# Row halves at the head of an attention and GeGLU kernel: half-width gate/up, and gate and up weights on two queues

## The chip, the cores and the metric

The kernel runs on one core of a Trainium2 chip. A core has a matmul engine (PE, whose weight loads are listed as PEld), a vector engine (DVE), an activation engine (ACT), GpSimd (POOL) and a sync engine (SP), which here only issues DMAs. The engines run side by side, each takes its own instructions in order, and they wait for each other by semaphores. ACT, POOL and SP can issue DMAs, and each of them has a queue of its own; 16 DMA engines work off the queues. The metric is the device time of one execution in microseconds (us): 560.81 as the median of 3 runs (560.77 to 560.82).

## What is computed

The input x has 2048 rows of 448 numbers. With xn = layernorm(x), the result is x + s * silu(g), where s is sliding attention over a key/value cache and g a gated feed-forward block:

```python
xn = _layernorm(x, axis=-1)
s = _A_ref(xn, A_k_cache, A_v_cache, A_wq, A_wo)   # 16 heads of 256, 8 KV heads, last 512 keys
g = _silu(_B_ref(xn, B_w_gate, B_w_up, B_w_down))  # (gelu(xn@w_gate) * (xn@w_up)) @ w_down, F = 1792
return x + s * g
```

Everything is bfloat16 with sums in float32.

## The kernel before, in words

The rows are taken in four chunks of 512 (`QC`), each of four tiles of 128 rows (`TPC`). Every operation goes through a recorder (`Rec`), which is told what an operation reads and writes, keeps the order in which each engine's operations were written, and adds the semaphore waits. So the order of the lines in the kernel is the order on each engine.

There are two stages. In the first, for each chunk, 14 blocks (`NF`) of 128 feed-forward columns run through `gate_up`, and then `down` multiplies by w_down for each of the four row tiles (the last chunk's `down` is put into the gaps of the second stage). The second stage goes over the 64 pairs of chunk and head: scores, softmax, values and output projection. It starts at about 127 us and the change does not touch it.

**`gate_up(c, f)`** (matmuls on line 370). 448 = 7 x 64, so the contraction runs in 7 steps (`NK`) of 64 rows (`HP`). The gate weights stand in partitions 0 to 63 of the tile `wgu`, the up weights in partitions 64 to 127, and the transposed rows `xnT` stand twice, once in either half. One step is two matmuls of 64 rows by 512 columns, one in each half of PE, into two neighbouring PSUM banks. There are three such pairs of banks (`NGB`), used in turn: block f+3 needs the banks of block f. ACT applies gelu to the gate bank (line 374), DVE multiplies the up bank by it (line 376) into `actT`.

**The head**, before the first `gate_up`. SP issues, in this order: the four row tiles of chunk 0; gate and up slices 0 and 1; the rows of chunk 1; gate and up slices 2 and 3; w_down; the rows of chunks 2 and 3. The slices are cut at blocks 0, 2, 6, 10 and 14, so slice 0 serves blocks 0 and 1. A gate slice is one DMA and an up slice another. DVE makes mean and variance of a row tile (lines 288 and 289), ACT the square root of two tiles together (line 330), DVE the reciprocal (line 333) and the normalised rows `xn2` (line 294), PE the 14 transposes of a tile (line 316), and ACT and DVE, tile by tile in turn, copy them from PSUM to `xnT` (lines 322 and 324). Ahead of its transposes PE runs 12 matmuls on zeroed data (`warm`, line 303), whose result nobody reads. A dummy square root on ACT (line 263) has its function table loaded early. Gelu needs another table, whose load stands ahead of the first gelu.

**Chunk 1's rows** are normalised while chunk 0 is in `gate_up`: `ln_later(t)` makes the statistics on DVE and the reciprocal root on POOL (lines 345 and 347), `ln_later2(t)` normalises on DVE and has the rows transposed by a DMA that SP issues (line 236). Eight such calls are hung behind blocks 4 to 11 (`lead = 4`), one behind each block's product, and behind blocks 1 to 8 for the chunks after. POOL also issues the loads of wq, V and wo (`load_piece`), from block 9 on, each after the matmul written last before it.

**`down(c, t)`** (line 382) is 14 matmuls, one for each block f, which reads block f of `actT`. PE takes them in order, so a late product stops it there.

```python
            lead = 4 if c == 0 else 1
            for f in range(NF):
                gate_up(c, f)
                if c + 1 < NQC and lead <= f < lead + 2 * TPC:
                    t, half = divmod(f - lead, 2)
                    (ln_later2 if half else ln_later)((c + 1) * TPC + t)
```

## Time and profile before

| | us |
|---|---|
| median of 3 runs | 560.81 (560.77 to 560.82) |
| the profiled execution | 561.18 |
| its span, first to last instruction | 559.4 |
| PE busy | 549.0 (98%) |
| DVE, ACT, POOL busy | 322.9, 296.1, 90.1 |
| first gate/up matmul starts | 9.26 |
| first down matmul starts | 30.91 |
| first row tile lands; up slices 0, 1, 2, 3 land | 2.77; 7.62, 12.54, 18.49, 22.54 |

Lines of a timeline read: start, duration, engine, line, operation, written tile<-read tiles, shapes, number of instructions merged, and in brackets the idle time of the engine before them with what ended it. A line with many instructions merged lasts from the start of the first to the end of the last. In a table of stretches each engine has its busy time and, in brackets, its number of instructions; the last three numbers are the granted PE clock (1.00 is full), the busy share of the DMA engines and GB/s. In the chain that ended last each piece has its start, its length and what it was.

### The profile page before, as it was taken

How to read it: one execution, taken by the hardware profiler on the slowest of the kernel's cores; microseconds unless marked ns; L12 is line 12 of the kernel's file. 1: busy time of each engine (PE TensorE's matmuls, PEld its weight loads, DVE VectorE, ACT ScalarE, POOL GpSimd, SP SyncE). 2: the span in 40 equal slices, each digit the busy share in tenths (PEclk: the TensorE clock that was granted, in tenths of full speed). 3: DMA queues.
4: the chain of work that ended last, by engine and by line, in shares of the span. 5: the costliest groups of instructions: out<-in, count | busy, mean ns of one | idle time of the engine just before them, and what ended most of it. 6: DMA issues, size and time to landing. Idle time of an engine off the chain costs nothing.

```text
span 559.4 us, 9865 instructions
## 1 busy us (share of the span) xinstructions
PE 549.0 (98%) x3499; PEld 257.2 (46%) x3532; DVE 322.9 (58%) x835; ACT 296.1 (53%) x673; POOL 90.1 (16%) x125
## 2 busy tenths in 40 slices
PE   7999999999999999999999999999999999999997
PEld 3544444444444444444444444444444444444445
DVE  5636446143464847474846657484747484755674
ACT  4324233247655565556565656656565656565641
POOL 0232323200000111013501101232100021400023
PEclk9999999999999999999999999999999999999999
DMA  8994746972453435353664344445535353645352
GB/s 193 276 191 86 138 102 136 247 137 65 94 85 68 97 64 99 69 91 64 143 98 94 73 86 71 81 84 137 101 67 99 63 95 71 147 79 101 70 92 52
DMA packets 169552, 58.83 MB, mean 105 GB/s; under 512 B 160160, under 2 KB 166432, under 8 KB 169504
## 3 DMA queue, kind: packets, MB, share of 16 engines
q1 hardware_dynamic: 166208, 45.50, 44.2%
q0 software_dynamic: 3152, 12.65, 8.9%
q8 instruction: 28, 0.46, 0.4%
q14 instruction: 20, 0.16, 0.1%
q10 hardware_dynamic: 144, 0.06, 0.0%
HBM read 17.92 MB, written 1.84 MB: 35 GB/s over the span
## 4 chain that ended last, share of the span: by engine, by line
PE 95%; DMA 1%; DVE 1%; issue 1%; SPq 1%; ACT 0%
PE ps L440 20%; PE ps L420 19%; PE ps L406 18%; PE ps L460 16%; PE ps L370 15%; PE ps L382 8%; DMA wgu<-in_B_w_up_dram 1%; SPq L233 1%; DVE tmp L469 0%; DVE ofin L471 0%; DVE pr L427 0%; DVE oT L446 0%; DVE rden L426 0%; ACT pr L424 0%
## 5 line engine op out<-in xcount | busy, mean ns | idle before, releaser
L424 ACT ACTIVATE pr<-ps 128x512 bf16<-128x512 f32 x256 | 152.8, 597 | 116.6 <-PE ps L420 112.5
L420 PE MATMUL ps<-kT,qT 128*128 128x512 bf16 x481 | 145.4, 379 | 3.3 <-issue 2.5
L440 PE MATMUL ps<-pT,V 128*128 128x512 bf16 x510 | 130.8, 379 | 0.6 <-DVE rden L426 0.4
L426 DVE RECIPROCAL rden<-den 128x1 f32<-128x1 f32 x256 | 41.5, 162 | 152.4 <-ACT pr L424 134.3
L460 PE MATMUL ps<-wo,oT 128*128 128x448 bf16 (+1 forms) x536 | 116.3, 344 | 0.0
L427 DVE TENSOR_SCALAR pr<-pr,rden 128x512 bf16<-128x512 bf16 x256 | 106.4, 416 | 9.0
L406 PE MATMUL ps<-xnT,wq 64*128 64x512 bf16 x896 | 99.5, 376 | 0.0
L410 ACT ACTIVATE qT<-ps 128x1024 bf16<-128x1024 f32 x64 | 65.5, 1024 | 49.8 <-PE ps L406 49.8
L370 PE MATMUL ps<-xnT,wgu 64*128 64x512 bf16 x784 | 85.5, 376 | 1.0 <-ACT xnT L322 0.8
L446 DVE CAST oT<-ps 128x512 bf16<-128x512 f32 x124 | 84.6, 682 | 0.6 <-PE ps L440 0.5
L440 PEld LDWEIGHTS ps<-pT,V 128*128 128x128 bf16 x512 | 49.9, 98 | 60.8 <-issue 1.2
L460 PEld LDWEIGHTS ps<-wo,oT 128*128 128x128 bf16 x536 | 52.3, 98 | 51.1
L420 PEld LDWEIGHTS ps<-kT,qT 128*128 128x128 bf16 x512 | 48.5, 98 | 57.1 <-issue 7.3
L376 DVE TENSOR_TENSOR actT<-ps,hb 128x512 bf16<-128x512 f32 x56 | 38.1, 685 | 57.5 <-ACT hb L374 55.7
L406 PEld LDWEIGHTS ps<-xnT,wq 64*128 64x128 bf16 x896 | 42.4, 94 | 55.9 <-DVE acc L481 4.2
L374 ACT ACTIVATE hb<-ps 128x512 bf16<-128x512 f32 x56 | 33.4, 597 | 51.8 <-PE ps L370 51.8
L370 PEld LDWEIGHTS ps<-xnT,wgu 64*128 64x128 bf16 x784 | 39.2, 94 | 46.5 <-issue 2.5
L424 ACT ACTIVATION_READ_ACCUMULATOR pr<-ps 128x1 f32 x256 | 49.9, 195 | 0.0
L500 POOL TENSOR_SCALAR tmp<-tmp 128x448 f32<-128x448 f32 x16 | 9.1, 572 | 233.9 <-ACT tmp L499 233.9
L382 PE MATMUL ps<-wd,actT 128*128 128x448 bf16 x224 | 46.2, 353 | 0.1
L485 POOL TENSOR_TENSOR tmp<-acc,gy 128x448 f32<-128x448 f32 x16 | 16.6, 1035 | 123.2 <-DVE acc L481 123.2
L382 PEld LDWEIGHTS ps<-wd,actT 128*128 128x128 bf16 x224 | 21.7, 98 | 22.2 <-issue 1.3
(43 smaller groups left out, 171.7 us busy)
## 6 DMA issues: line engine op xcount, KB each, us to landing
pT<-pr SPq DMA_TRANSPOSE x256, 2.4
wq<-in_A_wq_dram POOLq DMA_DIRECT2D x14, 256.0 KB, 4.3
wo<-in_A_wo_dram POOLq DMA_DIRECT2D x4, 896.0 KB, 10.1
V<-in_A_v_cache_dram POOLq DMA_DIRECT2D x4, 512.0 KB, 5.8
xr<-in_A_x_dram POOLq DMA_DIRECT2D x4, 448.0 KB, 4.8
wd<-in_B_w_down_dram SPq DMA_DIRECT2D x1, 1568.0 KB, 17.6
wgu<-in_B_w_gate_dram SPq DMA_DIRECT2D x3, 448.0 KB, 10.3
wgu<-in_B_w_up_dram SPq DMA_DIRECT2D x3, 448.0 KB, 11.8
```

Of the source, the lines that this page charges most:

```text
L370: ins = e.matmul(bank(b), lhsT=wgu[lo:lo + HP, k, f * P:(f + 1) * P], rhs=xnT[lo:lo + HP, c, k, :], start=k == 0, stop=k == NK - 1)
L376: dve(lambda e: e.tensor_tensor(actT[:, f, :], bank(s + 1), hb[:, n % NHB, :], ALU.mult), r=[("ps", s + 1), ("hb", n % NHB)], w=[("actT", f)])
L382: pe(lambda e, f=f: e.matmul(bank(b, D), lhsT=actT[:, f, t * P:(t + 1) * P], rhs=wd[:, f, :], start=f == 0, stop=f == NF - 1), r=[("actT", ...
L406: ins = e.matmul(bank(b), lhsT=wq[lo:lo + HP, k, h0 // 2 + hp, e_ * P:(e_ + 1) * P], rhs=xnT[lo:lo + HP, c, k, :], start=k == 0, stop=k == ...
L410: act(lambda e, e_=e_, s=s, i=i: e.activation(qT[:, i:i + 2, e_, :], psum[:, s * 512:(s + 2) * 512].rearrange("p (a q) -> p a q", a=2), AC ...
L420: ins = e.matmul(bank(b), lhsT=qT[:, i % 6, k, t * P:(t + 1) * P], rhs=kT[:, g, k, :], start=k == 0, stop=k == NE - 1)
L424: act(lambda e: e.activation(pr[s][:, :], bank(b), ACT.Exp, scale=scale, accum_out=den[:, s:s + 1]), r=[("ps", b)], w=[("pr%d" % s,), ("de ...
L426: dve(lambda e: e.reciprocal(rden[:, s:s + 1], den[:, s:s + 1]), r=[("den", s)], w=[("rden", s)])
L427: dve(lambda e: e.tensor_scalar(pr[s][:, :], pr[s][:, :], rden[:, s:s + 1], None, op0=ALU.mult), r=[("pr%d" % s,), ("rden", s)], w=[("pr%d ...
L440: ins = e.matmul(bank(b), lhsT=V[:, j, g, e_ * P:(e_ + 1) * P], rhs=pT[:, i % NPT, j, :], start=j == 0, stop=j == NJ - 1)
L446: dve(lambda e: e.tensor_copy(dst, bank(b)), r=[("ps", b)], w=[key])
L460: ins = e.matmul(bank(b, D)[:, lo:hi], lhsT=oT[G % 2][:, idx, t * P:(t + 1) * P], rhs=wo[:, h0 * NE + idx, lo:hi], start=idx == 0, stop=id ...
```

## The change

Chunk 0's rows are handled in two halves of 256.

- **Rows.** Tiles 0 and 1 are normalised, transposed and copied first, and each tile gets its own square root. The statistics of tile 2 stand between the two copies, and those of tile 3 behind them. The transposes and copies of tiles 2 and 3 stand, in PE's, ACT's and DVE's order, behind the first two half blocks.
- **Half-width gate/up.** Blocks 0, 1 and 2 first run on columns 0 to 255 of `xnT` and later on columns 256 to 511, into the same PSUM banks; gelu and product come once, after the second half. The order on PE is: first half of blocks 0 and 1, transposes of tiles 2 and 3, first half of block 2, second halves of blocks 0, 1 and 2, and then whole blocks from 3 on.
- **Loads.** The slices are cut at 0, 2, 4, 6, 10 and 14. Gate slices stay on SP, up slices go to ACT's queue: 0 and 1 ahead of the square roots, 2 and 3 behind the first two, 4 behind the third. Row tile 3 also goes to ACT's queue, behind POOL's making of the identity matrix. Chunk 1's rows come after gate slice 3.
- **Gelu's table.** A dummy gelu on ACT stands behind the fourth square root and ahead of the copy of tile 2.
- **Warming matmuls.** 36 and later 6 of 128 columns in place of 12 of 512; the zeroed tile shrinks with them.
- **Chunk 1's normalisation** is hung behind blocks 5 to 12 (`lead = 5`).

```diff
@@ -236,35 +236,41 @@
             return R.op("sync", lambda e: e.dma_start_transpose(dst, src), r=r, w=w, dma=True, after=after, lane=lane)
 
 
-        dve(lambda e: e.memset(actT[:, NF - 1, :], 0.0), w=[("actT", NF - 1)])
+        dve(lambda e: e.memset(actT[:, NF - 1, 0:P], 0.0), w=[("actT", NF - 1)])
         pool(lambda e: e.memset(small[:, 0:1], LN_EPS), w=[("eps",)])
         pool(lambda e: e.memset(small[:, 1:2], -0.5), w=[("mhalf",)])
         pool(lambda e: e.memset(ident[:, :], 0.0), w=[("ident",)])
-        pool(lambda e: e.affine_select(out=ident[:, :], in_=ident[:, :], compare_op=ALU.not_equal,
-                                       fill=1.0, base=0, pattern=[[-1, P]], channel_multiplier=1),
-             r=[("ident",)], w=[("ident",)])
-
-
-        x0 = [dma("sync", x4[:, t, :], x_view[:, 0, t, :], w=[("x4", t)]) for t in range(TPC)]
+        made = pool(lambda e: e.affine_select(out=ident[:, :], in_=ident[:, :], compare_op=ALU.not_equal,
+                                              fill=1.0, base=0, pattern=[[-1, P]], channel_multiplier=1),
+                    r=[("ident",)], w=[("ident",)])
+
+
+        for t in range(TPC - 1):
+            dma("sync", x4[:, t, :], x_view[:, 0, t, :], w=[("x4", t)])
         wg_v = B_wg.rearrange("(k p) f -> p k f", p=HP)
         wu_v = B_wu.rearrange("(k p) f -> p k f", p=HP)
-        cuts = [0, 2, 6, 10, NF]
-        fslice = {f: s for s in range(4) for f in range(cuts[s], cuts[s + 1])}
-
-        def load_gu(s):
+        cuts = [0, 2, 4, 6, 10, NF]
+        fslice = {f: s for s in range(5) for f in range(cuts[s], cuts[s + 1])}
+
+        def load_gu(s, eng):
             a, b = cuts[s] * P, cuts[s + 1] * P
-            dma("sync", wgu[0:HP, :, a:b], wg_v[:, :, a:b], w=[("wgu", 0, s)])
-            dma("sync", wgu[HP:P, :, a:b], wu_v[:, :, a:b], w=[("wgu", 1, s)])
+            if eng == "sync":
+                dma(eng, wgu[0:HP, :, a:b], wg_v[:, :, a:b], w=[("wgu", 0, s)])
+            else:
+                dma(eng, wgu[HP:P, :, a:b], wu_v[:, :, a:b], w=[("wgu", 1, s)])
 
         def load_x(c):
             dma("sync", x4[:, c * TPC:(c + 1) * TPC, :], x_view[:, c, :, :],
                 w=[("x4", c * TPC + t) for t in range(TPC)])
 
         act(lambda e: e.activation(small[:, 2:3], small[:, 0:1], ACT.Sqrt), r=[("eps",)], w=[("warm",)])
-        for sl in range(4):
-            load_gu(sl)
-            if sl == 1:
+        dma("scalar", x4[:, TPC - 1, :], x_view[:, 0, TPC - 1, :], w=[("x4", TPC - 1)], after=[made])
+        for sl in range(5):
+            load_gu(sl, "sync")
+            if sl == 3:
                 load_x(1)
+        load_gu(0, "scalar")
+        load_gu(1, "scalar")
         dma("sync", wd[:, :, :], B_wd.rearrange("(f p) d -> p f d", p=P), w=[("wd",)])
         for c in range(2, NQC):
             load_x(c)
@@ -300,44 +306,57 @@
 
             def run(e):
                 for _ in range(n):
-                    ins = e.matmul(bank(3), lhsT=actT[:, NF - 1, 0:P], rhs=actT[:, NF - 1, :], start=True, stop=True)
+                    ins = e.matmul(bank(3, P), lhsT=actT[:, NF - 1, 0:P], rhs=actT[:, NF - 1, 0:P], start=True, stop=True)
                 return ins
             pe(run, r=[("actT", NF - 1)], w=[("ps", 3)])
 
+        def ln_std(t):
+            act(lambda e: e.activation(std[:, t:t + 1], mv[:, t:t + 1, 1], ACT.Sqrt, bias=small[:, 0:1]),
+                r=[("mv", t), ("eps",)], w=[("std", t)])
+
+        def ln_first(t):
+            dve(lambda e: e.reciprocal(rstd[:, t:t + 1], std[:, t:t + 1]), r=[("std", t)], w=[("rstd", t)])
+            ln_norm(t, 1)
+
         def ln_tr(t):
-            parts = ((act, 4),), ((dve, 5),), ((act, 6),), ((dve, 7),)
-            parts = [(eng, b, 0, NK) for eng, b in parts[t]]
-            for eng, b, a, z in parts:
-                tp = bank(b).bitcast(BF16)
-
-                def tr(e, tp=tp, a=a, z=z):
-                    for k in range(a, z):
-                        for lo in (0, HP):
-                            ins = e.transpose(tp[lo:lo + HP, (k - a) * P:(k - a + 1) * P], xn2[:, t, k, 0, :], ident[:, :])
-                    return ins
-                pe(tr, r=[("xn2", t, 0), ("ident",)], w=[("ps", b)])
-                dst = xnT[:, 0, a:z, t * P:(t + 1) * P]
-                src = tp[:, 0:(z - a) * P].rearrange("p (k q) -> p k q", q=P)
-                if eng is act:
-                    act(lambda e, dst=dst, src=src: e.activation(dst, src, ACT.Copy), r=[("ps", b)], w=[("xnT", 0, t, a)])
-                else:
-                    dve(lambda e, dst=dst, src=src: e.tensor_copy(dst, src), r=[("ps", b)], w=[("xnT", 0, t, a)])
-
-        for t in range(TPC):
+            tp = bank(6 + t % 2).bitcast(BF16)
+
+            def tr(e):
+                for k in range(NK):
+                    for lo in (0, HP):
+                        ins = e.transpose(tp[lo:lo + HP, k * P:(k + 1) * P], xn2[:, t, k, 0, :], ident[:, :])
+                return ins
+            pe(tr, r=[("xn2", t, 0), ("ident",)], w=[("ps", 6 + t % 2)])
+
+        def ln_copy(t):
+            dst = xnT[:, 0, :, t * P:(t + 1) * P]
+            src = bank(6 + t % 2).bitcast(BF16)[:, 0:NK * P].rearrange("p (k q) -> p k q", q=P)
+            if t % 2:
+                dve(lambda e: e.tensor_copy(dst, src), r=[("ps", 6 + t % 2)], w=[("xnT", 0, t)])
+            else:
+                act(lambda e: e.activation(dst, src, ACT.Copy), r=[("ps", 6 + t % 2)], w=[("xnT", 0, t)])
+
+
+        warm(36)
+        for t in range(2):
             ln_stats(t)
-            if t % 2:
-                a, b = t - 1, t + 1
-                act(lambda e, a=a, b=b: e.activation(std[:, a:b], mv[:, a:b, 1], ACT.Sqrt, bias=small[:, 0:1]),
-                    r=[("mv", a), ("mv", t), ("eps",)], w=[("std", a)])
-        for a in range(0, TPC, 2):
-            dve(lambda e, a=a: e.reciprocal(rstd[:, a:a + 2], std[:, a:a + 2]),
-                r=[("std", a)], w=[("rstd", a), ("rstd", a + 1)])
-            ln_norm(a, 1)
-            ln_norm(a + 1, 1)
-        warm(12)
-        for t in range(TPC):
+            ln_std(t)
+        load_gu(2, "scalar")
+        load_gu(3, "scalar")
+        for t in range(2):
+            ln_first(t)
             ln_tr(t)
-        xn0 = [("xnT", 0, t, 0) for t in range(TPC)]
+        warm(6)
+        ln_copy(0)
+        ln_stats(2)
+        ln_copy(1)
+        ln_std(2)
+        load_gu(4, "scalar")
+        ln_stats(3)
+        ln_std(3)
+        act(lambda e: e.activation(small[:, 2:3], small[:, 0:1], ACT.Gelu_apprx_tanh), r=[("eps",)], w=[("warm",)])
+        for t in range(2, TPC):
+            ln_first(t)
 
         def ln_later(t):
 
@@ -354,12 +373,12 @@
                  r=[("xn2", t % NX, 0), ("xn2", t % NX, 1)], w=[("xnT", c, t4)])
 
         def xn(c):
-            return [("xnT", c, t) for t in range(TPC)] if c else xn0
+            return [("xnT", c, t) for t in range(TPC)]
 
 
         NGB = 3
 
-        def gate_up(c, f):
+        def gate_up(c, f, q0=0, q1=QC):
 
             n = c * NF + f
             s = 2 * (n % NGB)
@@ -367,10 +386,12 @@
             def run(e):
                 for k in range(NK):
                     for b, lo in ((s, 0), (s + 1, HP)):
-                        ins = e.matmul(bank(b), lhsT=wgu[lo:lo + HP, k, f * P:(f + 1) * P],
-                                       rhs=xnT[lo:lo + HP, c, k, :], start=k == 0, stop=k == NK - 1)
+                        ins = e.matmul(bank(b)[:, q0:q1], lhsT=wgu[lo:lo + HP, k, f * P:(f + 1) * P],
+                                       rhs=xnT[lo:lo + HP, c, k, q0:q1], start=k == 0, stop=k == NK - 1)
                 return ins
-            pe(run, r=xn(c) + [("wgu", 0, fslice[f]), ("wgu", 1, fslice[f])], w=[("ps", s), ("ps", s + 1)])
+            pe(run, r=xn(c)[q0 // P:q1 // P] + [("wgu", 0, fslice[f]), ("wgu", 1, fslice[f])], w=[("ps", s), ("ps", s + 1)])
+            if q1 < QC:
+                return
             act(lambda e: e.activation(hb[:, n % NHB, :], bank(s), ACT.Gelu_apprx_tanh),
                 r=[("ps", s)], w=[("hb", n % NHB)])
             dve(lambda e: e.tensor_tensor(actT[:, f, :], bank(s + 1), hb[:, n % NHB, :], ALU.mult),
@@ -504,9 +525,16 @@
 
 
         for c in range(NQC):
-            lead = 4 if c == 0 else 1
+            lead = 5 if c == 0 else 1
+            if c == 0:
+                for f in range(NGB):
+                    gate_up(0, f, 0, QC // 2)
+                    if f == 1:
+                        for t in range(2, TPC):
+                            ln_tr(t)
+                            ln_copy(t)
             for f in range(NF):
-                gate_up(c, f)
+                gate_up(c, f, QC // 2 if c == 0 and f < NGB else 0)
                 if c + 1 < NQC and lead <= f < lead + 2 * TPC:
                     t, half = divmod(f - lead, 2)
                     (ln_later2 if half else ln_later)((c + 1) * TPC + t)
```

## The prediction

> **What bounds the kernel now.** I read the busy line of the page first, then the chain that ended last in order of time, then the timeline of the first 35 us, because the diff touches nothing later.
>
> ```profile
> PE 549.0 (98%) x3499; PEld 257.2 (46%) x3532; DVE 322.9 (58%) x835; ACT 296.1 (53%) x673; POOL 90.1 (16%) x125
> ```
> ```profile
> 4.70 7.84 DMA wgu<-in_B_w_up_dram
> 12.67 18.31 PE ps L370 x168
> 30.98 10.70 PE ps L382 x56
> ```
>
> PE is busy 98% of 559.4 us. The lost time is the head, before the first gate/up matmul. From 12.67 us one gate/up block costs 18.31/12 = 1.526 us. So a microsecond won at the head reaches the end, unless something later is tied to another clock.
>
> ```profile
> 9.26 3.20 PE L370 MATMUL ps<-xnT,wgu 64*128 64x512 bf16 x28 [0.77 <-ACT xnT L322]
> 12.67 7.51 PE L370 MATMUL ps<-xnT,wgu 64*128 64x512 bf16 x68 [0.22 <-DMA wgu<-in_B_w_up_dram]
> ```
>
> PE's timeline: the first block starts at 9.26, released by the last row copy, not by a weight; the third waits 0.22 for its up weights. The fourth starts at 12.67 + 1.53 = 14.20. What happens ahead of 9.26:
>
> ```profile
> 5.91 0.92 DVE L294 TENSOR_SCALAR xn<-x,mv,rstd 128x448 bf16<-128x448 bf16 x2
> ...
> 6.47 2.02 PE L316 MATMUL ps<-ident,xn 128*64 128x128 bf16 x56 [1.09 <-DVE xn L294]
> ...
> 7.09 1.94 ACT L322 ACTIVATE xnT<-ps 128x896 bf16<-128x896 bf16 x2 [0.94 <-PE ps L316]
> ...
> 7.77 1.39 DVE L324 COPY xnT<-ps 128x896 bf16<-128x896 bf16 x2
> ...
> 9.05 1.28 ACT L374 ACT_TABLE_LOAD   x1
> ```
>
> DVE does four statistics, then four normalisations, then two of the four copies. The gelu table load (9.05 to 10.33) lies beside the first block, so it costs nothing now. Last, the place where the head meets the next stage:
>
> ```profile
> 29.50 0.67 DVE L376 TENSOR_TENSOR actT<-ps,hb 128x512 bf16<-128x512 f32 x1
> 30.66 0.92 DVE L294 TENSOR_SCALAR xn<-x,mv,rstd 128x448 bf16<-128x448 bf16 x2 [0.49 <-POOL rstd L347]
> 31.50 1.28 DVE L376 TENSOR_TENSOR actT<-ps,hb 128x512 bf16<-128x512 f32 x2
> ```
> ```profile
> 30.91 3.39 PE L382 MATMUL ps<-wd,actT 128*128 128x448 bf16 x17
> ```
>
> DVE is late here: the last product of chunk 0 ends at 32.78, while PE has been in the down projection since 30.91.
>
> **The change, part by part.**
>
> *Rows.* DVE now does statistics 0 and 1, normalises 0 and 1, statistics 2, copy 1. The first x tile lands at 2.77. A statistics pair takes 0.73 of DVE (starts 3.56, 4.29), so the first reciprocal can start at 4.29. Reciprocal to normalisation is 0.17 (5.74 to 5.91): 4.46 to 4.96. The second needs its square root: aggregate ends 4.37, ACT 0.30, hand-over 0.11, so reciprocal 4.87, normalisation 5.06 to 5.56. Transposes of tile 1 follow at 5.63, and from a tile's first transpose to its copy the trace has 0.62 (6.47 to 7.09): copy 1 could start at 6.25, behind statistics 2 (5.48 to 6.21), and ends at 6.88. PE starts 0.07 after a DVE copy: 6.95. ACT's copy 0 (0.92) must fit by then.
>
> *DMA issues put on ACT.* Six of them (tile 3 of x, five up slices). On SP one costs 0.43 for an x tile and 0.63 to 0.73 for a slice; I take the same on ACT (its one issue in this trace, a 56 KB store, took 0.38). If ACT's sequencer issues while the first table load runs, two up slices are out by 3.4 and the square roots are not late; slices 2 and 3 go out from 4.4 to 5.7, copy 0 runs 5.8 to 6.7, and PE starts at 6.95. If issues wait for the engine, everything on ACT is 0.7 later (first free at 2.22): square root 0 at 4.07, copy 0 from 6.13 to 7.05, PE at 7.12. Should issues from two sequencers slow each other to 1.3 each, copy 0 ends near 8.1. I take 7.05.
>
> *Half-width gate/up.* The narrowest matmul with a full weight load, 128x224 in the last projection, steps 96 ns, or 0.428 ns a column; 256 columns then step 110 ns, and seven pairs take 0.77. Two halves are 1.54 against 1.526: three blocks cost 0.04 more. Loads could break this, two per 110 ns; the transposes load 64 columns every 28 ns, so 128 columns every 56, which just fits. Bounds: 0 and 0.3.
>
> *Rows 256 to 511.* PE runs halves of blocks 0 and 1 (7.05 to 8.59), transposes 2 and 3 (0.41 each, to 9.4), half of block 2 (to 10.2), then needs copies 2 and 3. On ACT square root 3 comes after statistics 3 (DVE 6.8 to 7.65): 7.7 to 8.0, or 8.3 if the last up issue is in the way. Then **the gelu table load, 1.28, plus its dummy activation, 0.20, now stand ahead of copy 2**: 9.5 to 9.8, copy 2 0.92, ending 10.4 to 10.75. PE resumes at 10.65, an idle 0.4 to 0.5. The early table read thus costs this 0.45 instead of saving: before it was covered by block 0.
>
> *Block 3* reuses the PSUM pair of block 0, so it waits for block 0's gelu and product: the seven pairs end at 11.6, gelu 0.60, product 0.69, with three hand-overs 0.2: 13.1. Block 3 starts at 13.05, against 14.20: **gain 1.15** (0.9 to 1.35 by the two ACT cases).
>
> *Weights.* While gate and up slices land, the core moves 208 to 220 GB/s with the engines full; when the down weights land, 338:
>
> ```profile
> 13.00:19.00 6.00, 6.00 (x60) 3.11 (x57) 2.95 (x5) 1.95 (x5) 0.00 (x0) 1.00 1.14 208
> 22.00:25.00 3.00, 3.00 (x32) 1.55 (x30) 2.48 (x7) 1.17 (x3) 0.80 (x2) 1.00 1.10 338
> ```
>
> A slice goes to 64 partitions, the down weights to 128, the packets being about the same (1,024 and 896 bytes). At 220 GB/s from 3.6 us: slice 0 plus x is 0.92 MB, and a landing trails the bytes by 1 to 1.5 us (up slice 0: issued 3.36, landed 7.62, 4.26). Issued at 2.0 to 2.7 instead, it lands 6.3 to 7.0, just in time; slice 1 near 9, needed at 9.4; slice 3 by 16, needed at 17.6; x of chunk 1 by 17, needed at 18.5. The 0.22 wait is gone; it is inside the 1.15.
>
> [...]
>
> *Lead 4 becomes 5.* Chunk 1's normalisation is hung one block later, and this is paid at the end. From the product of block 4 (18.12) to the start of that of block 12 (31.50) DVE and POOL run one chain of 13.38: two blocks take 3.34 there, against 3.05 on PE. It now starts with the product of block 5, 19.63 less the gain, so block 13's product starts at 33.01 and ends at 33.69 less the gain. PE wants it for the fourteenth down matmul, 30.91 + 13 x 0.19 = 33.38 less the gain. **PE waits 0.37** with the hand-over of 0.06; before it had 0.6 to spare. Nothing later wins that back. The last transposed rows of chunk 1 are issued at 31.6 + 1.5 - 1.2 = 31.9 and land 7.3 later, 39.2, needed at 40.9.
>
> *Warm matmuls, memset.* 36 of 128 columns: 0.107 each at half clock (the 512 ones step 0.427) from 1.05, full clock from 4.14 as now, done by about 4.6; if loads don't hide (0.15 each), 5.5, which costs 0.1 on copy 0. Fewer DMAs on SP let the down weights start earlier; they land at 27.2 now, needed at 29.8.
>
> **Sum:** -1.15 + 0.37 = -0.8 us. The profiled execution took 561.18 (span 559.4, 1.78 around it), 0.37 above the median; its steps are fixed latencies, so I take the difference off the median: 560.81 - 0.8 = 560.0. What a measurement can tell from no change is 0.2%, or 1.12 us, so 559.69 to 561.93 is "the same".
>
> **The rivals.**
>
> *The wait at the down projection doesn't come, or PE starts earlier.* If ACT issues overlap fully (gain 1.35) and POOL is quicker once the loads are out of the way, net 1.2 to 1.5: 559.4, just faster. For it: 0.49 of each normalisation's wait is POOL's. Against: that chain is made of the same instructions as before. 28%.
>
> *ACT issues slow each other, or up slice 0 lands late.* Each microsecond at copy 0 costs 0.8 to 1 of the gain; copy 0 at 8.1 leaves nothing: 560.8, still "the same". 15%.
>
> *Slower: ACT's issue blocks on a full queue.*
>
> ```profile
> 9.52 2.73 SPq L233 DMA_DIRECT2D wd<-in_B_w_down_dram  x1
> 12.28 9.57 SPq L233 DMA_DIRECT2D x<-in_A_x_dram  x2
> ```
>
> On SP a blocked issue holds nothing but loads. On ACT, square roots and copies stand behind it. If up slice 3 or 4 blocked as the down weights' issue did (2.7, so 2.0 more than free), copy 0 or 2 would be 2 late; from 2 us of blocking on, the sum is past zero by more than 1.12: 3 of blocking gives 563.0. Against: SP took twelve issues, 3.7 MB, before the first slow one at 8.07; ACT gets six, 1.7 MB. 10%.
>
> **How the numbers follow.** The forecast itself (net 0.3 to 1.1) has 47%, so "the same" is 47 + 15 = 62%, faster 28%, slower 10%. The range goes from the faster case's middle, 559.3, to 561.0, which takes in the lost-gain case and leaves out the blocked queue and the far end of faster; its own range alone would be 559.7 to 560.5.
>
> **What would show it.** Right: first half-width matmul at 6.9 to 7.2, released by a row copy; a table load near 8.1 between square root 3 and copy 2 and an idle PE of about 0.4 ahead of the second half of block 0; block 3 at 13.0; a PE wait of 0.3 to 0.4 on a product inside the first down projection. Wrong: PE waiting on up weights at its first block, an ACT issue over 1.3, half blocks of over 0.9, or no wait at the down projection.

## The result and the profile after

The changed kernel takes 562.35 us (median of 10 runs, 561.75 to 563.83) against 560.95 for the kernel before in the same comparison (10 runs): a ratio of 1.0022, with a 95% interval from 1.0012 to 1.0032. It is slower by 1.4 us between the medians, 1.2 by the ratio; I had forecast 0.8 us less. The span went from 559.4 to 560.8.

The page's busy line and two pieces of the chain that ended last, for the changed kernel:

```profile
PE 549.6 (98%) x3571; PEld 261.5 (47%) x3604; DVE 323.7 (58%) x837; ACT 296.5 (53%) x676; POOL 90.1 (16%) x125
```
```profile
2.12 6.38 DMA wgu<-in_B_w_gate_dram
8.74 1.70 PE ps L389 x28
```

PE's work grew by 0.6 us, the span by 1.4. The chain now begins with gate slice 0, issued at 2.12 and landed at 8.50. PE's timeline shows where the time went:

```profile
6.30 0.51 PE L309 MATMUL ps<-actT 128*128 128x128 bf16 x6
8.74 1.70 PE L389 MATMUL ps<-xnT,wgu 64*128 64x256 bf16 x28 [1.94 <-DMA wgu<-in_B_w_gate_dram]
...
11.28 5.09 PE L389 MATMUL ps<-xnT,wgu 64*128 64x256 bf16 x70
17.00 15.57 PE L389 MATMUL ps<-xnT,wgu 64*128 64x512 bf16 x140 [0.63 <-ACT hb L395]
32.50 10.86 PE L403 MATMUL ps<-wd,actT 128*128 128x448 bf16 x56
43.30 1.90 PE L389 MATMUL ps<-xnT,wgu 64*128 64x512 bf16 x16
```

The first half block waits 1.94 for a weight. A second wait stands before 17.00, ahead of block 4; the line puts it down to ACT, but ACT's gelu of block 3 runs from 16.41 to 17.01, past the start, and the PSUM banks that block 4 needs, those of block 1, were free by 16.06, when DVE had ended the products of blocks 0 to 2. Up slice 2 landed at 16.86; that DMA is what ended the wait. A third, of 0.29, is hidden inside the same line: block 6 starts at 20.31, 1.80 behind block 5 instead of 1.51, just after up slice 3 landed at 20.17. When the main events happen, from the two timelines:

| | before | after | later by |
|---|---|---|---|
| first gate/up matmul | 9.26 | 8.74 | -0.52 |
| block 3 | 14.18 | 14.69 | 0.51 |
| block 4 | 15.69 | 17.00 | 1.31 |
| first down matmul | 30.91 | 32.50 | 1.59 |
| chunk 1's first gate/up matmul | 41.61 | 43.30 | 1.69 |
| second stage, first matmul | 126.69 | 128.37 | 1.68 |
| last matmul | 556.03 | 557.39 | 1.36 |

Everything lost is lost in the first 43 us. The second stage, which is the same program, took 0.32 less than in the one profile of before, whose run lay 0.37 above that kernel's first median; I count this as spread between executions.

The rows were not late. ACT's timeline after the change, with the DMA issues that it now carries:

```profile
1.55 0.40 ACTq L233 DMA_DIRECT2D x<-in_A_x_dram  x1
2.00 0.69 ACTq L233 DMA_DIRECT2D wgu<-in_B_w_up_dram  x1
...
4.57 1.40 ACTq L233 DMA_DIRECT2D wgu<-in_B_w_up_dram  x2
6.01 0.92 ACT L337 ACTIVATE xnT<-ps 128x896 bf16<-128x896 bf16 x1 [1.16 <-PE ps L327]
...
8.13 1.28 ACT L357 ACT_TABLE_LOAD   x1
...
11.00 0.92 ACT L337 ACTIVATE xnT<-ps 128x896 bf16<-128x896 bf16 x1 [1.37 <-PE ps L327]
```

Copy 0 ends at 6.93 and DVE's copy 1 at 7.03, so the rows would have let PE start at 7.10. The slices, as issued and as landed (engine that issued the up slice in brackets; all gate slices are SP's). The cuts differ: from slice 1 on a slice of one number serves other blocks before than after.

| slice | gate before | up before | gate after | up after |
|---|---|---|---|---|
| 0 | 2.59, 6.19 | 3.36, 7.62 | 2.12, 8.50 | 2.00, 6.70 (ACT) |
| 1 | 4.03, 10.29 | 4.70, 12.54 | 2.89, 10.05 | 2.72, 8.95 (ACT) |
| 2 | 6.04, 16.36 | 6.68, 18.49 | 3.68, 11.26 | 4.57, 16.86 (ACT) |
| 3 | 7.35, 20.62 | 8.07, 22.54 | 4.36, 13.74 | 5.21, 20.17 (ACT) |
| 4 | | | 5.70, 18.52 | 6.52, 23.29 (ACT) |

In slices 0 and 1 the up half comes first, by 1.8 and 1.1 us; in slices 2 and 3 the gate half does, by 5.6 and 6.4; and a block needs both. Gate slice 0 takes 6.4 us from issue to landing instead of 3.6. And ACT's queue, with up slice 2 issued at 4.57, moved almost nothing from 7.2 to 9.5 us (0.01 MB). The table of stretches gives the rate:

```profile
7.00:9.50 2.50, 0.76 (x14) 0.79 (x16) 1.88 (x7) 1.76 (x4) 0.00 (x0) 1.00 1.23 190
...
15.00:19.00 4.00, 3.37 (x34) 1.58 (x31) 1.68 (x3) 1.14 (x3) 0.00 (x0) 1.00 1.11 292
```

190 GB/s while nearly all of it is gate slices, 292 later, with gate and up slices on the two queues and, towards the end, the down weights. From 15.5 to 16.0, with gate slice 4 and up slice 3 alone, it is 348. The size of the packets is not the reason: the old kernel, with gate and up slices of 1,024-byte packets one after the other, moved 208 (the prediction's row for 13 to 19 us). What makes the slower rows slow is not shown; the 348 is what the two halves reached side by side here. The kernel just doesn't get them side by side when it needs them.

### The profile page after: what moved, and what is told of

Its sections match the earlier page's. It is cut to its first block, busy times and chain, and to the rows that moved or that the text cites. A ratio compares the mean times of both kernels' runs of the same rounds, so it can differ in the third digit from the quotient of the medians.

```text
span 560.8 us, 10021 instructions
## 1 busy us (share of the span) xinstructions
PE 549.6 (98%) x3571; PEld 261.5 (47%) x3604; DVE 323.7 (58%) x837; ACT 296.5 (53%) x676; POOL 90.1 (16%) x125
## 4 chain that ended last, share of the span: by engine, by line
PE 96%; DVE 1%; DMA 1%; issue 1%; SPq 0%; ACT 0%
PE ps L461 20%; PE ps L441 19%; PE ps L427 18%; PE ps L481 16%; PE ps L389 15%; PE ps L403 8%; DMA wgu<-in_B_w_gate_dram 1%; DVE tmp L490 0%; DVE ofin L492 0%; SPq L233 0%; DVE pr L448 0%; PE ps L327 0%; ACT hb L395 0%; DVE oT L467 0%; DVE rden L447 0%
## 5 line engine op out<-in xcount | busy, mean ns | idle before, releaser
L389 PE MATMUL ps<-xnT,wgu 64*128 64x512 bf16 (+1 forms) x826 | 86.2, 365 | 2.7 <-DMA wgu<-in_B_w_gate_dram 1.9
L389 PEld LDWEIGHTS ps<-xnT,wgu 64*128 64x128 bf16 x826 | 41.1, 94 | 46.9 <-issue 3.3
```

The costliest lines, as they stand in the source:

```text
L389: ins = e.matmul(bank(b)[:, q0:q1], lhsT=wgu[lo:lo + HP, k, f * P:(f + 1) * P], rhs=xnT[lo:lo + HP, c, k, q0:q1], start=k == 0, stop=k == ...
```

## The experiments

Two theories stood at first. **Theory 1:** what SP and ACT issue is made ready in one common order of issue, so up slice 2 stands behind gate slice 3. **Theory 2:** the two queues are not to blame, or each queue simply gets its share of the DMA engines.

### One queue again

```diff
+            dma(eng, wgu[0:HP, :, a:b], wg_v[:, :, a:b], w=[("wgu", 0, s)])
+            dma(eng, wgu[HP:P, :, a:b], wu_v[:, :, a:b], w=[("wgu", 1, s)])
...
-        load_gu(0, "scalar")
-        load_gu(1, "scalar")
...
-        load_gu(2, "scalar")
-        load_gu(3, "scalar")
...
-        load_gu(4, "scalar")
```

> The changed kernel with the up slices put back on SP, each right behind its gate slice; cuts, row halves, table and lead stay as changed. Theory 1 (transfers that SP and ACT issue are made ready in the one order in which they were issued, so up slice 2, issued at 4.57 behind gate slice 3 at 4.36, moved its first bytes at 9.5): gate and up of a slice now stand next to each other; up slice 0 lands near 7.2, slice 1 by 9.3, slice 2 by 11.5, slice 3 by 16; the first half block starts near 7.2 instead of 8.74, block 4 doesn't wait, block 3 starts near 13.1 and the down projection waits up to 0.4: about 2.4 us less than the changed kernel, 560.0. Theory 2 (two queues do no harm; smaller slices and their 512-byte packets make slice 0 late, and the half blocks the rest): slice 0 still lands at 8 or later, block 4 still waits, time within 0.5 of the changed kernel, 562.

Measured: 560.72 us, ratio to before 0.9987 (0.9966 to 1.0008). Gate and up slice 0 landed at 6.06 and 7.23, slice 1 by 9.47, slice 2 by 11.73, slice 3 by 17.23. PE's timeline:

```profile
7.37 1.71 PE L382 MATMUL ps<-xnT,wgu 64*128 64x256 bf16 x28 [0.43 <-DMA wgu<-in_B_w_up_dram]
...
9.90 20.20 PE L382 MATMUL ps<-xnT,wgu 64*128 64x256 bf16 x210
30.04 2.63 PE L396 MATMUL ps<-wd,actT 128*128 128x448 bf16 x13
33.17 2.07 PE L396 MATMUL ps<-wd,actT 128*128 128x448 bf16 x10 [0.50 <-DVE actT L390]
```

The first wait shrinks to 0.43, the one of block 4 is gone, and block 3 starts at 13.31, 0.87 before the old kernel's and 1.38 before the changed one's. The first down matmul gains 0.87 on before. Then the wait that the prediction named appears: the fourteenth down matmul waits for the product of block 13, 0.66 (starts 0.85 apart instead of 0.19). It is larger than the 0.37 worked out, because chunk 1's rows landed only at 19.64 and the normalisation began that much later. The two queues are the loss. Of the rest of the change 0.2 us is left at the start of the second stage (126.49 against 126.69, one profile each); in the times this kernel can't be told from the one before.

### Gate slice 3 issued 0.4 us later

```diff
+        load_rest([R.ops["scalar"][-1]])
         load_gu(2, "scalar")
         load_gu(3, "scalar")
```

`load_rest` has SP issue gate slice 3, chunk 1's rows, gate slice 4, w_down and the rows of chunks 2 and 3, behind the operation given.

> The changed kernel, in which SP issues gate slice 3 and all that follows only after the square root of tile 1, which is after ACT could go on to issue up slice 2. Theory 1 (one order of issue for both queues): up slice 2 goes ahead of gate slice 3 and lands near 12 to 13 instead of 16.86; the 0.8 wait of block 4 is gone, the late first block (8.74) stays: about 0.8 to 1.0 less than the changed kernel, 561.4. Theory 2 (each queue has its own way and the DMA engines give ACT's queue less while SP's has much to do): up slice 2 lands within 1.5 of 16.9, block 4 still waits, time as changed, 562.3.

Measured: 561.00 us, ratio 0.999 (0.997 to 1.001). Gate slice 3 went out at 4.72, after up slice 2 at 4.41. Up slice 2 landed at 12.53 instead of 16.86, and there is no wait at block 4 any more:

```profile
7.75 1.71 PE L392 MATMUL ps<-xnT,wgu 64*128 64x256 bf16 x28 [1.10 <-DVE rstd L320]
...
10.29 20.20 PE L392 MATMUL ps<-xnT,wgu 64*128 64x256 bf16 x210
30.42 2.63 PE L406 MATMUL ps<-wd,actT 128*128 128x448 bf16 x13
33.25 8.31 PE L406 MATMUL ps<-wd,actT 128*128 128x448 bf16 x43 [0.20 <-DVE actT L400]
```

Changing the order by 0.36 us of issue moved a landing by 4.3 us: for up slice 2 this is what theory 1 expected, and theory 2 did not. Not expected was the first block, which started at 7.75 instead of 8.74: gate slice 0 landed at 7.50 instead of 8.50, though nothing that is issued ahead of it had moved. The wait for the product of block 13 is 0.36 here, against 0.37 in the prediction.

### Up slice 2 issued 1.2 us sooner

```diff
         load_gu(1, "scalar")
+        load_gu(2, "scalar")
...
-        load_gu(2, "scalar")
```

> The changed kernel with one DMA moved on ACT: up slice 2 is issued behind up slice 1, ahead of the first square root (about 3.4 in place of 4.57), so ahead of gate slices 2 and 3. Theory 1: it lands with them, near 11 to 12 in place of 16.86; block 4 does not wait. Up slice 3 stays behind gate slice 3 and what SP issues, landing 18 to 20. The first block is as late as in the changed kernel or later, for up slices 1 and 2 now both compete with gate slice 0: 8.7 to 9.3. Theory 2 (ACT's queue gets less of the engines while SP's is full): up slice 2 lands only 1.2 sooner, as it is issued 1.2 sooner, near 15.7.

Measured: 561.42 us in one run. Up slice 2, issued at 3.39, landed at 11.29, 5.6 sooner; block 4 doesn't wait, and the first down matmul starts at 31.06 instead of 32.50. It is the same result from the other side. Gate slice 0 landed at 8.15. Up slice 3, issued at 4.45, behind gate slice 3, landed at 17.55.

### Up slices on POOL's queue

```diff
-        load_gu(0, "scalar")
-        load_gu(1, "scalar")
+        for sl in range(5):
+            load_gu(sl, "gpsimd")
```

> The changed kernel with all up slices issued by POOL, one after the other from about 1.6 us, instead of ACT. [...] Theory 1: what holds up slice 2 back is the order of issue shared by SP and ACT; on POOL's queue it moves as soon as up slice 1 is through, from 7 or 8 us, and lands by 11 to 12; gate and up are loaded together at 260 GB/s or more throughout; block 4 doesn't wait. The first block starts between 7.2 and 8.7: 560.0 to 561.5. Theory 2 (sharing of the engines): a second queue of any kind lets the later up slices take bytes from gate slice 0, which lands at 8.5 or later again, and up slices lag behind the gate slices later: 562 or more.

Measured: 561.56 us, ratio 1.0009 (0.9985 to 1.0033). Up slices landed at 6.08, 8.58, 10.28, 14.01 and 16.59, as theory 1 has it. But this doesn't show that POOL's queue stands outside the common order: POOL issued up slices 2, 3 and 4 at 3.40, 4.11 and 4.82, each ahead of its gate slice (3.55, 4.23, 5.57), and an order common to all three engines would bring them early too. Gate and up together moved 238 to 248 GB/s between 10 and 18 us, less than the 260 I expected. And gate slice 0 landed at 8.83, the first block started at 9.07:

```profile
9.07 3.12 PE L386 MATMUL ps<-xnT,wgu 64*128 64x256 bf16 x28 [2.14 <-DMA wgu<-in_B_w_gate_dram]
```

So the late gate slice 0 is not a matter of the order of issue, and theory 1 explains only the second and third wait. In this profiled run the first blocks also ran at half speed (3.12 us instead of 1.70), of which more below.

### The old loads under the new order of work

```diff
-        for t in range(TPC - 1):
+        for t in range(TPC):
...
-        cuts = [0, 2, 4, 6, 10, NF]
+        cuts = [0, 2, 6, 10, NF]
...
+            dma(eng, wgu[0:HP, :, a:b], wg_v[:, :, a:b], w=[("wgu", 0, s)])
+            dma(eng, wgu[HP:P, :, a:b], wu_v[:, :, a:b], w=[("wgu", 1, s)])
...
-            if sl == 3:
+            if sl == 1:
                 load_x(1)
```

> The changed kernel with the loads of the kernel before: all four row tiles and all slices on SP, cut at 0, 2, 6, 10, 14, chunk 1's rows behind slice 1. What is left is the change of the order of work. Theory 1: slice 0 lands at 7.6 as before, so the first half block starts at 7.7; up slice 1, which serves block 2, lands at 12.5 as before, and the half of block 2, wanted at 10.1, waits until 12.6; block 3 starts at about 15.7, 1.5 later than before: 562.0 to 562.5, with the wait named as up slice 1. If the row order alone were at fault (theory 2), the first block would start late too, at 8.5 or after.

Measured: 563.61 us, ratio 1.0037 (1.0015 to 1.0059). In five of the ten runs, those of 564 us and more, the granted clock was 0.996 or 0.997; the other five took 562.32 to 563.14.

```profile
7.50 1.70 PE L381 MATMUL ps<-xnT,wgu 64*128 64x256 bf16 x28 [0.71 <-DMA wgu<-in_B_w_up_dram]
...
11.98 20.08 PE L381 MATMUL ps<-xnT,wgu 64*128 64x256 bf16 x210 [1.87 <-DMA wgu<-in_B_w_up_dram]
```

The first block starts early, and the half of block 2 waits 1.87 for up slice 1. So the finer cuts are needed: an earlier start only helps if the next weights come earlier too.

### What holds up gate slice 0

First, whether up slice 1 passes it on the other queue:

```diff
         load_gu(0, "scalar")
-        load_gu(1, "scalar")
...
+        load_gu(1, "scalar")
         load_gu(2, "scalar")
```

> The changed kernel with one DMA moved the other way: up slice 1 is issued by ACT only behind the square root of tile 1 (4.45 in place of 2.72), after gate slices 1 to 3. So while gate slice 0 loads, ACT's queue holds only row tile 3 and up slice 0. In every run with the up slices of blocks 0 to 3 on a second queue gate slice 0 landed at 7.5 to 10.1, in every run with them on SP at 6.1 to 6.3. Theory A (up slice 1, on the other queue, takes bytes ahead of gate slice 0): gate slice 0 lands at 6.2 to 7.0, the first block starts at 7.1 to 7.2 on its rows. Theory B (a second queue alone delays it, or gate slices 1 to 3 behind it on SP do): 7.5 or later again. In both, up slice 1 comes behind gate slice 3 (order of issue) and lands at 13 or later, the half of block 2 waits 3 or more for it, and the kernel is slower than the changed one: 563 to 565.

Measured: 566.43 us, ratio 1.0093 (1.0076 to 1.011). Gate slice 0 landed at 8.02 all the same, so theory A, with its 6.2 to 7.0, falls. The half of block 2 started at 14.70, waiting for up slice 1, which landed at 14.56. The time is above the 563 to 565 I gave, because PE also ran at a lower clock (below). Then the two things that remained, each by itself:

```diff
-            dma(eng, wgu[HP:P, :, a:b], wu_v[:, :, a:b], w=[("wgu", 1, s)])
+            dma("scalar" if s == 0 else eng, wgu[HP:P, :, a:b], wu_v[:, :, a:b], w=[("wgu", 1, s)])
```

(an edit of the one-queue kernel)

> e1_up_on_sp with up slice 0 alone on ACT's queue, issued at 2.0 as in the changed kernel; on SP follow gate slices 0 and 1, up 1, gate 2, up 2 and so on. If a second queue by itself holds up gate slice 0, it lands at 7.5 or later as in the changed kernel, and the first block starts 0.3 or more later than in e1 (7.37). If it was the row of gate slices behind it on SP, it lands by 6.6, up slice 0 by 6.6, and the first block starts on its rows, 7.05 to 7.15, 0.2 to 0.3 sooner than in e1.

```diff
+        for sl in (0, 1, 2, -1, -2, -3, 3, -4, 4, -5):
+            load_gu(sl)
```

(-1 stands for up slice 0, -2 for up slice 1, and so on; all of them on SP, and ACT carries only the row tile)

> The changed kernel with all slices on SP, in the order gate 0, 1, 2, up 0, 1, 2, gate 3, up 3, chunk 1's rows, gate 4, up 4. There is no second queue. If gate slices standing behind each other on one queue hold up the first of them, gate slice 0 lands at 7.5 or later; if the second queue does it, gate slice 0 lands at 6.1 to 6.3 as with one queue in turn. Up slice 0 is behind three gate slices in both cases and lands near 10.5 to 11, so block 0 starts there and the kernel is slower than the changed one by 1 to 4.

Measured: with up slice 0 alone on ACT's queue gate slice 0 landed at 7.62 and the first block started at 7.86 (561.04 us, ratio 0.9997, 0.9978 to 1.0017). With one queue and three gate slices in a row it landed at 6.75, between the two answers that I had expected (565.55 us in one run; block 0 waits for up slice 0, which landed at 10.33). So a single slice on a second queue is enough to delay gate slice 0, by 1.56 us over the one-queue run (6.06), and the row of gate slices, without a second queue, makes 0.69. In the run with up slice 0 on ACT's queue the row tiles came later too (the second at 3.86 instead of 3.29), and PE's first block was released by its rows.

Each of these is one profile, and with two queues the landing varies much: in the run with gate slice 3 later it was 7.50, in the last run below 10.09, though both kernels issue the same loads in the same order and within 0.03 us of each other up to gate slice 3. So whether the row of gate slices adds anything to what the second queue does is not shown. What holds over the fourteen profiles other than that with the gate slices in a row is the gap: gate slice 0 landed at 6.06 to 6.30 in the seven where SP alternated gate and up and ACT carried at most row tile 3 and up slices of later blocks, and at 7.50 to 10.09 in the seven where any of the up slices of blocks 0 to 3 stood on a second queue. How the DMA engines share two queues is not visible in these traces; that part stays open.

### The early gelu table

```diff
-        act(lambda e: e.activation(small[:, 2:3], small[:, 0:1], ACT.Gelu_apprx_tanh), r=[("eps",)], w=[("warm",)])
```

(an edit of the one-queue kernel)

> e1_up_on_sp without the dummy gelu, so that gelu's table is loaded ahead of the first real gelu. The prediction priced the early load at 0.45, standing ahead of the copy of row tile 2. If so, that copy ends about 0.4 sooner and block 3 starts that much sooner. But in e1_up_on_sp the load and its dummy were over at 9.75, while the transposes of tile 2 ended near 9.6, so the copy could hardly start sooner: then block 3 starts within 0.1 of 13.31, or later by what the first gelu is late.

Measured: 560.61 us in one run. ACT's timeline:

```profile
9.67 0.92 ACT L333 ACTIVATE xnT<-ps 128x896 bf16<-128x896 bf16 x1 [1.28 <-PE ps L323]
10.61 1.28 ACT L387 ACT_TABLE_LOAD   x1
11.90 1.27 ACT L387 ACTIVATE hb<-ps 128x512 bf16<-128x512 f32 x2
```

Without the early load the copy of tile 2 starts at 9.67; with it, at 9.66. Block 3 starts at 13.45 here and at 13.31 with the early load. In these two profiles the early table costs nothing; it may bring 0.1, since PE's wait before block 3 is that much longer here.

### Mending it

Slices 0 and 1 in turn on SP, the later ones side by side, and the lead back at 4:

```diff
-            else:
+            if eng == "scalar" or s < 2:
                 dma(eng, wgu[HP:P, :, a:b], wu_v[:, :, a:b], w=[("wgu", 1, s)])
...
-        load_gu(0, "scalar")
-        load_gu(1, "scalar")
...
-            lead = 5 if c == 0 else 1
+            lead = 4 if c == 0 else 1
```

> The changed kernel with up slices 0 and 1 on SP behind their gate slices, slices 2 to 4 left side by side on ACT's and SP's queue (up 2 is then issued near 4.5, ahead of gate 2 at 4.9), and the lead back at 4. Theory 1 (order of issue): now every up slice is issued next to its gate slice, so up slice 2 lands by 12, and from there gate and up load together at near 300 GB/s: slice 3 by 15.5, chunk 1's rows by 17, slice 4 by 20. No wait but the first: 560.0, 0.8 to 0.9 under the kernel before. Theory 2 (two queues cost whatever the order): slice 0 or 2 late again, a wait at block 0 or 4 of 0.5 and more, 561 or above.

Measured: 562.48 us, ratio 1.0016 (1.0004 to 1.0027). Up slice 2 landed at 10.52 and up slice 3 at 14.50, with 290 GB/s from 14 to 18 us; but gate slice 3 came only at 17.20, where I had expected the whole slice by 15.5. Up slice 1, on SP, landed at 10.78 and the half of block 2 waited 0.80 for it; and chunk 1's rows came at 19.64, too late for a lead of 4. Up slice 2 on the second queue came in ahead of up slice 1 on the first, which had been issued sooner. I take this for the same effect that delays gate slice 0, but no run here tests it for up slice 1.

One queue, chunk 1's rows behind slice 2, slice 3 cut in two, lead 4:

```diff
-        cuts = [0, 2, 4, 6, 10, NF]
+        cuts = [0, 2, 4, 6, 8, 10, NF]
...
-            if sl == 3:
+            if sl == 2:
                 load_x(1)
...
-            lead = 5 if c == 0 else 1
+            lead = 4 if c == 0 else 1
```

> Up slices back on SP as in e1_up_on_sp, slice 3 cut into blocks 6-7 and 8-9, chunk 1's rows right behind slice 2, and chunk 1's normalisation hung behind blocks 4 to 11 again. In e1_up_on_sp the down projection waited 0.5 to 0.66 for the product of block 13, because chunk 1's rows landed at 19.64 and the chain began one block later. If that wait is due to the lead and the late rows, it goes: rows land near 14, no wait inside the down projection, first block at 7.3 to 7.4, the first down matmul at 30.0 as there, and the second stage starts 0.6 sooner than with e1_up_on_sp: about 560.1, 0.8 under the kernel before. If block 13 is late for another reason, the wait stays and the time is that of e1_up_on_sp.

Measured: 560.71 us (559.95 to 567.12), ratio 1.0013 (0.9988 to 1.0039). Two of the twelve runs took 566.51 and 567.12 us at a granted clock of 0.994. The wait in the down projection is gone, and a new one stands behind it:

```profile
30.12 10.77 PE L396 MATMUL ps<-wd,actT 128*128 128x448 bf16 x56
42.35 2.98 PE L382 MATMUL ps<-xnT,wgu 64*128 64x512 bf16 x26 [1.46 <-DMA xnT<-xn]
```

The last transpose of chunk 1's rows, issued at 31.2, landed at 42.2. With the rows of chunks 2 and 3 moved behind those transposes in SP's queue:

```diff
-        for c in range(2, NQC):
-            load_x(c)
...
+            if c == 0:
+                load_x(2)
+                load_x(3)
             for g in ((0, 1), (2, 3, 4), (5, 6, 7), ())[c]:
```

> e5_rows_earlier_lead4 with the rows of chunks 2 and 3 issued by SP only behind the four transposes of chunk 1's rows. In e5 the wait in the down projection was gone, but the next stage waited 1.46 for the last transpose, issued at 31.2 and landed at 42.2: the four transposes stand in SP's queue behind the down weights and the rows of chunks 2 and 3, which landed at 29.0 and 30.3. If that queue is the cause, the transposes land 2 to 4 sooner, the last by 38 to 39, no PE wait is left after the first block, and the second stage starts 0.8 to 0.9 sooner than in the kernel before: 560.0. If the cause is what comes after them (loads of wq by POOL, 28.0 to 40), the last transpose lands past 41 again and the time is 560.7 or more.

Measured: 560.35 us (560.04 to 561.06) against 561.27, ratio 0.9984 (0.9975 to 0.9993).

```profile
7.56 1.70 PE L379 MATMUL ps<-xnT,wgu 64*128 64x256 bf16 x28 [0.76 <-DVE stats L287]
...
10.10 20.20 PE L379 MATMUL ps<-xnT,wgu 64*128 64x256 bf16 x210
30.23 10.77 PE L393 MATMUL ps<-wd,actT 128*128 128x448 bf16 x56
40.93 5.35 PE L379 MATMUL ps<-xnT,wgu 64*128 64x512 bf16 x48
```

The last transpose landed at 36.10, and from the first block to here the timeline lists no PE wait. The second stage starts at 126.00, 0.69 before the old kernel and 2.37 before the changed one. This version is 0.16% faster than the kernel before, with an interval below 1, and so ahead of the changed one too.

Lead 4 and the rows of chunks 2 and 3 moved in the same way, in the two-queue kernel with gate slice 3 behind up slice 2:

```diff
+            if c == 0:
+                load_x(2)
+                load_x(3)
...
-            lead = 5 if c == 0 else 1
+            lead = 4 if c == 0 else 1
```

> e2_gate3_later (two queues, gate slice 3 issued behind up slice 2) with the lead back at 4 and the rows of chunks 2 and 3 behind chunk 1's transposes. In e2 the wait for the product of block 13 took 0.36 in the down projection (starts 0.55 apart in place of 0.19). With the chain begun one block sooner it goes, as chunk 1's rows land at 16.4, before block 4's product; the first down matmul stays at 30.4: 0.4 to 0.5 under the kernel before, 560.4. If two queues with the order mended were as good as one, the first block would start at 7.4 as with one queue; e2 had 7.75, and I expect 7.7 again.

Measured: 561.28 us (560.21 to 565.40), ratio 1.0009 (0.9991 to 1.0026). The profiled execution was a bad one, 565.40: gate slice 0 landed at 10.09, and

```profile
10.34 3.17 PE L389 MATMUL ps<-xnT,wgu 64*128 64x256 bf16 x28 [3.68 <-DMA wgu<-in_B_w_gate_dram]
```
```profile
10.00:20.00 10.00, 9.61 (x127) 7.38 (x129) 2.70 (x4) 2.71 (x4) 0.00 (x0) 0.74 1.12 271
```

The 28 half-width matmuls took 3.17 us instead of 1.70, and the granted clock of PE (the third number from the end) fell to 0.74 over that stretch. In five of the twelve runs the clock was 0.994 to 0.997, and those took 562.47 us and more. Two queues were thus not as good as one here even with the order mended (561.28 against 560.35 beside the same runs of the kernel before), and less steady than that one-queue version, none of whose eleven runs lost clock. The two kernels also differ in the cut of slice 3 and the place of chunk 1's rows, and the one-queue version before it had two such runs in twelve, so the queues may not be all of it.

## Why the prediction was wrong

**Right: rows.** PE's rows were there at 7.03, and the prediction had 6.88 to 7.05; the 0.15 above 6.88 is mostly the second x tile, which landed at 3.66 instead of 3.25.

**Right: issues on ACT.** They took 0.40 to 0.76 each, started at 1.55 while the table load ran, and held up no square root and no copy for long. The rival in which an issue on ACT blocks didn't come.

**Right: half-width matmuls.** They step 109 ns (8.744, 8.853, 8.961), against 110 ns.

**Wrong: the weights.** This is the step that failed. "At 220 GB/s from 3.6 us" treated the slices as one stream that delivers slice 0, then 1, then 2, whichever queue carries them, and took the landing time of up slice 0 for both halves of a slice. Its figures do not meet either: 0.92 MB at 220 GB/s from 3.6 us end at 7.8, while the 6.3 to 7.0 is the new time of issue plus the 4.26 of the old up slice 0. Up slice 0 landed at 6.70, inside the 6.3 to 7.0; gate slice 0 at 8.50, at least 2.2 later than in any profile with one queue in turn (6.06 to 6.30), because of the second queue. Slice 2 was not even given a time, and its up half landed at 16.86, because ACT issues it behind SP's gate slice 3: issued ahead of that, it landed at 11.29 and 12.53. Slice 3, given for 16, had its up half at 20.17. Together: block 0 waits 1.64 beyond its rows, block 4 0.80, block 6 0.29. Why a second queue delays the first slice of the other stays open.

The rival "ACT issues slow each other, or up slice 0 lands late" had the right kind of cause, but named the wrong slice, had 15%, and ended at 560.8: it priced a late copy 0, at 8.1, and did not see that the later slices are late as well. The slower case that I did price, a blocked queue, is not what happened.

**Wrong: the early gelu table.** The 0.45 was not paid; but no run started PE at the 7.05 it was worked out for, so what it would have cost there is not shown. With the first block at 7.4 or later the transposes of tile 2 end when the table load does, and in the changed kernel 1.4 us after it.

**Right, but covered here: the lead of 5.** The wait of 0.37 in the down projection was 0.08 in the changed kernel (starts 0.27 apart instead of 0.19), since the waits of blocks 4 and 6 had given DVE time. As soon as the weights are in order it is there: 0.36 with gate slice 3 later, 0.35 without the early table, and 0.66 with one queue, where chunk 1's rows were late as well.

**The sum.** With one queue the prediction's -1.15 for block 3 measures -0.87 (the old kernel's block 3 starts at 14.18, not 14.20, as its blocks step 1.51 us, not 1.526), for PE still waited for up slice 0 there and started at 7.37, not 7.05; and its +0.37 measures 0.35 to 0.66. So row halves, table and lead by themselves came near what was said of each, but not to the 0.8 that was forecast for the sum: 0.2 was left at the second stage. The two queues took 1.4 at block 3 and 1.1 behind it.

That a second queue leaves the waits as worked out was my estimate. The runs are worse than that: the second queue did not only bring nothing at the first block, it delayed what was already first in line (gate slice 0 at 8.50 in the changed kernel, at 6.06 with one queue).

## What to carry to other kernels

A consumer that needs two transfers was served here by issuing the two next to each other (both halves of slice 2 by 11.73 with one queue). Queues of their own did not put them side by side (gate slice 2 at 11.26, up slice 2 at 16.86), and the earlier issuer ran ahead with what nobody needed yet (gate slice 3, for block 6, at 13.74). When a start is moved forward, work out the landing of every transfer that the next microseconds need, in the order in which SP and ACT together issue them, and not only of the first. And a step that is hung one place later has to be followed to where its stage ends: here it came back in the down projection (0.35 to 0.66), and behind that a wait stood at the last transposes (1.46).

## What the runs showed of the hardware

**Across SP and ACT it mattered who issued first.** Up slice 2 landed at 16.86 when ACT issued it 0.21 after gate slice 3, at 12.53 when 0.31 ahead of it, and at 11.29 when 0.97 ahead. It was not a strict order of landing: in the changed kernel chunk 1's rows, issued by SP 0.47 behind up slice 2, landed 1.2 ahead of it, and gate slice 4, issued 0.49 behind up slice 3, 1.65 ahead of that. Whether POOL stands outside this order is not shown. One landing speaks for it: up slice 4 from POOL was issued 0.59 behind gate slice 3 and landed 1.25 ahead of it.

**In some runs a wait of PE cost more than its length.** In 2 of the 10 runs of the changed kernel the mean granted clock was 0.997 instead of 1.0, and they took 563.07 and 563.83 us, among the three slowest of the ten. In the last one-queue version it was 1.000 in all 11, in the one before that 0.994 in 2 of 12. In the profiles the drop was seen behind waits of 2.14, 3.68 and 3.72 us, where the 28 half-width matmuls took 3.12, 3.17 and 3.17 us instead of 1.70, but also in the run with up slice 1 later, where PE had waited only 1.50 before its first block and still took 3.06 us for the 28 half-width matmuls:

```profile
8.27 3.06 PE L389 MATMUL ps<-xnT,wgu 64*128 64x256 bf16 x28 [1.50 <-ACT std L313]
```

After 1.58 (up slice 2 sooner), 1.87 (old loads) and 1.94 (the changed kernel) there was no drop, so the length of the wait alone doesn't decide. In the run with up slice 1 later the granted clock changed in steps of 3.41 us: full from 5.02, half from 8.43, full from 11.85, half from 15.26 and full from 18.67. What makes it drop after one wait and not after another is not shown.

**Gate and up slices one after the other moved at 190 to 244 GB/s, side by side at up to 348.** The 190 is from the stretch in which gate slices ran nearly alone. With one queue, where gate and up follow each other, it was 208 (13 to 19 us) and 220 (6 to 9) in the kernel before, and 244 (4 to 6), 228 (6 to 8) and 221 (10 to 14) without the early table. On SP's and ACT's queue together, mixed with other loads, it was 258 (9.5 to 15 us) and 292 (15 to 19) in the changed kernel, and 348 in the half microsecond with gate slice 4 and up slice 3 alone; with the up slices on POOL's queue 238 to 248.
